# From block 3 on VectorE transposes q in 32x32 blocks, and x is made on 32x64 tiles of the TensorE array

## The chip, the core and the metric

One core of one Trainium2 chip. Its engines run on their own and meet through semaphores: TensorE (PE: matmuls; PEld: its weight loads), VectorE (DVE), ScalarE (ACT), GpSimd (POOL), and SyncE (SP), whose queue issues the transfers (DMA). The metric is device time in microseconds of one execution, as the median of several.

## What is computed

Attention of a linear kind, then a feed-forward layer:

```
q_s  = exp(q - max_d(q)) / sum_d                       # softmax over the 64 features
k_s  = exp(k - max_s(k)) / sum_s                       # softmax over the 576 positions
kv   = einsum('bhsd,bhse->bhde', k_s, v)               # 64x64 for each batch and head
x    = einsum('bhsd,bhde->bhse', q_s, kv)  -> (4608, 512)
out  = (h * sigmoid(1.702 h)) @ w_out,  h = x @ w_in   # 512 -> 2048 -> 512
```

There are 8 batches, 8 heads, 576 positions and 64 features. q, k and v are float32; the weights come as 64-bit floats and are split on the chip into two float32 parts.

## The kernel before

The 4608 tokens are cut into 12 blocks of 384 (TB), so that three blocks make two batches. A partition p of the 128 holds three tokens in a row (c = 0..2). Every other block of the later ones has tokens of two batches; `parts(t)` gives the one or two pieces.

For a block, **q** is loaded for one pair of heads at a time (`load_q`, from block 2 on into two buffers qt), made a softmax (`q_soft`: VectorE L532 maximum and L533 subtraction, ScalarE L536 exp, VectorE L539 to L542 sum, reciprocal and product), and turned so that features lie on partitions: `q_tr` has three TensorE transposes (L584) into a PSUM bank, and ScalarE copies them to qT (L591).

For a batch, **k** is made a softmax (`k_max`, `k_sub`), and `kv_pairs` multiplies it with v on TensorE (L494, 64 columns of the array for each head of a pair, 65 columns of data: the last is the sum). VectorE forms the reciprocals r (L499, L500), and ScalarE writes the scaled 64x64 blocks into kvn (L510), eight for a batch.

**x** is made by `x_pairs`. In blocks 0 to 2 it is one matmul of the full 128x128 array a head pair (L630), against kvn with zeros off the diagonal. From block 3 on all four head pairs go together on the four 64x64 tiles of the array (L635): four 64x64 products of two pairs fill the four tiles. For that, every second pair has its two heads exchanged (`turned`), which costs `load_q` two transfers in place of one. x is then split into a high and a low part, xh on ScalarE (L599) and xl on VectorE (L602).

**The feed-forward layer** is 16 steps a block: `g1` (L659: 12 matmuls of 384 columns, from xh, xl and two parts of w_in), gelu and a cast on ScalarE (L665, L668), the low part gl on VectorE (L671), and `g2` (L691: nine matmuls of 512 columns into three PSUM banks). g2 follows its g1 by two steps. The three results of a block are copied to tmp (L704) and stored (L707).

**The order** of every engine's list is fixed beforehand by a planner (`Plan`): each piece of work has a cost, the buffers that it reads and writes, and a rank; at each engine the ready piece of lowest rank goes next. The kernel then emits the pieces in that order, and each engine runs its list strictly in it. For blocks 2 and on, the ranks of loads, softmax, transposes and x are set by `n0(i)`, the sixteenths of the block ahead of it.

The weights' split (`conv_w`, L276 to L295) fills the first 150 us on VectorE and ScalarE. Early inputs of batches 0 and 1 lie in places where weights come later.

Of the kernel before, what the change touches and what calls it, by code (L numbers as in the profile page):

```python
# [131 lines left out]
def efficient_attention_then_gelu_ffn(  # L132
# [13 lines left out]
    nc = tc.nc  # L146
# [16 lines left out]
    QACT = set()  # L163
# [11 lines left out]
    kvn = [sb(f"kvn{i}", [P, NP, P]) for i in range(2)]  # L175
    xs = [[sb(f"x{s}{i}", [P, NP, TB], F32R) for s in "hl"] for i in range(2)]
    g = [sb(f"g{i}", [P, TB]) for i in range(3)]
# [5 lines left out]
    qt_ = [sb(f"qt{i}", [P, C, 2, D]) for i in range(2)]  # L183
    mx_ = [sb(f"mx{i}", [P, 2, D]) for i in range(2)]
# [4 lines left out]
    first = sb("first", [P, D])  # L189
    nc.vector.memset(first, 0.0)  # L190
    nc.gpsimd.partition_all_reduce(first, first, P, bass_isa.ReduceOp.max)
    for t in kvn:
        nc.vector.memset(t, 0.0)
# [3 lines left out]
    def zero_tail(kl, vl):  # L197
        nc.vector.memset(kl[ST:P], 0.0)
        nc.vector.memset(vl[ST:P], 0.0)
        nc.vector.memset(vl[:, :, D:W], 1.0)  # L200

    zero_tail(*tail[0])
    one = sb("one", [P, 1])
    nc.vector.memset(one, 1.0)
# [9 lines left out]
    for gr in range(2):  # L214
# [11 lines left out]
    et, _ = early("wi10", "et", [P, H * (D + W)], 0)  # L226
    etail[0] = (
        et[:, : H * D].rearrange("p (h d) -> p h d", h=H),
        et[:, H * D : H * (D + W)].rearrange("p (h d) -> p h d", h=H),
# [154 lines left out]
    def turned(b, hp):  # L384


        return b > 1 and hp % 2 == 1

    def load_q(t, i, rank):
        n = group(t)  # L390
        qt, key = eq[t, i] if t < 2 else (qt_[i % 2], ("qt", i % 2))
        qbuf[t, i] = qt, key
        runs = [(0, 1, 1), (1, 0, 1)] if turned(parts(t)[0][0], i) else [(0, 0, n)]

        def run():
            for b, s0, p0, p1 in parts(t):
                for o, h, m in runs:
                    src = q[b, n * i + h : n * i + h + m, s0 : s0 + (p1 - p0) * C, :]
                    if t < 2:
                        nc.sync.dma_start(  # L400
                            out=qt[p0:p1].rearrange("p h c d -> p h (c d)"),
                            in_=src.rearrange("h (p c) d -> p h (c d)", c=C),
                        )
                    else:
                        nc.sync.dma_start(
                            out=qt[p0:p1, :, o : o + m], in_=src.rearrange("h (p c) d -> p c h d", c=C)
                        )

        plan.add("SP", plan.ISSUE * len(parts(t)) * len(runs), behind(t > 1), (key,), rank, run, size=n * TB * D * 4)
# [4 lines left out]
    def k_max(b, i, rank):  # L414
# [4 lines left out]
        s = nm[0] % 2  # L419
# [48 lines left out]
    def kv_pairs(b, hps, t, rank):  # L468
# [12 lines left out]
        def run():  # L481
            for m, hp in enumerate(hps):
                i, o = divmod(2 * hp, n)
                kt, vt = kbuf[b, i][0], vbuf[b, i][0]

                for cols in (slice(0, D), slice(D, W)) if b < 2 else (slice(0, W),):
                    for c in range(CM + 1):
                        for a in range(2):
                            lhs = kt[:, o + a, c, :] if c < CM else kl[:, 2 * hp + a, :]
                            rhs = vt[:, o + a, c, :] if c < CM else vl[:, 2 * hp + a, cols]  # L490
                            if cols.start == D:
                                rhs = vl[:, 2 * hp + a, cols] if c == CM else one
                            r0 = (a ^ turned(b, hp)) * D
                            nc.tensor.matmul(  # L494
                                pk[r0 : r0 + D, m, cols], lhs, rhs, start=c == 0, stop=c == CM, tile_position=(0, r0)
                            )
# [7 lines left out]
        plan.add("DVE", 0.35, (PB,), (R,), rank, run_r)  # L504
        for m, hp in enumerate(hps):

            def run_n(m=m, hp=hp):
                for a in range(2):
                    rows, cols = (slice(x * D, (x + 1) * D) for x in (a ^ turned(b, hp), a))
                    nc.scalar.mul(kvn[b % 2][rows, hp, cols], pk[rows, m, 0:D], r[rows, m : m + 1])  # L510

            plan.add("ACT", 0.65, (PB, R), (("kvn", b % 2, hp),), rank, run_n)
# [3 lines left out]
    sums = [sb(f"qs{i}", [P, 4 * C]) for i in range(2)]  # L516
    qm = [sb(f"qm{i}", [P, 4 * C]) for i in range(2)]

    def q_soft(t, i, ranks):
# [25 lines left out]
        if (t, i) in QACT:  # L545

            flat = qt.rearrange("p h c d -> p (h c d)")
            mf, sf = qm[i % 2], sums[i % 2]

            def run_n():  # L550
                nc.vector.tensor_reduce(out=m, in_=qt, axis=AX.X, op=ALU.max, negate=True)

            def run_a():
                for x in range(n * C):
                    w = flat[:, x * D : (x + 1) * D]
                    nc.scalar.activation(w, w, AF.Exp, bias=mf[:, x : x + 1], accum_out=sf[:, x : x + 1])

            def run_z():
                nc.vector.tensor_scalar_add(sf, sf, 1e-9)
                nc.vector.reciprocal(sf, sf)  # L560
                nc.vector.tensor_tensor(
                    out=dst, in0=qt, in1=bc(sf.rearrange("p (h c) -> p h c", h=n), D), op=ALU.mult
                )

            Q = ("qs", i % 2)
            plan.add("DVE", dve(e), (key,), (M,), ranks[0], run_n)
            plan.add("ACT", 0.30 * n * C, (key, M), (key, Q), ranks[1], run_a, table="exp")
            plan.add("DVE", dve(e) + 0.4, (key, Q), (nkey, Q), ranks[2], run_z)
            return
# [5 lines left out]
    def q_tr(t, hp, rank):  # L575
        n = group(t)
        i, o = divmod(2 * hp, n)
        qt, key = qbuf[t, i]
        bk = next_bank(t)
# [8 lines left out]
        qT, Q = qTs[hp], ("qT", hp)  # L588

# [5 lines left out]
    def x_out(t, hp, px, PB, rank):  # L595
        xh, xl = (x[:, hp, :] for x in xs[t % 2])

        def run_h():
            nc.scalar.copy(xh, px[:, :TB])  # L599

        def run_l():
            nc.vector.tensor_tensor(out=xl, in0=px[:, :TB], in1=xh.bitcast(F32), op=ALU.subtract)  # L602

        X = ("x", t % 2)
        plan.add("ACT", act(TB), (PB,), ((*X, "h", hp),), rank, run_h)
        plan.add("DVE", dve(TB), (PB, (*X, "h", hp)), ((*X, "l", hp),), rank, run_l)

    def x_pairs(t, hps, rank):


        bks = [next_bank(t) for _ in hps[-3:]]
        if len(hps) > 3:

            bks.insert(0, 6 + (ng[0] + 1) % 2)
        reads = []
        for hp in hps:
            reads.append(("qT", hp))
            reads += [("kvn", b % 2, hp) for b, *_ in parts(t)]

        def run():  # L620
            for b, s0, p0, p1 in parts(t):
                todo = []
                for hp, bk in zip(hps, bks):
                    qx, po = (
                        y[:, :TB].rearrange("a (c p) -> a c p", c=C)[:, :, p0:p1] for y in (qTs[hp], bank[bk])
                    )
                    todo.append((po, kvn[b % 2][:, hp, :], qx, hp % 2))
                if len(hps) == 1:
                    (po, kx, qx, _), = todo
                    nc.tensor.matmul(po, kx, qx, start=True, stop=True)  # L630
                    continue
                for pair, a in ((y, a) for y in range(0, len(todo), 2) for a in range(2)):
                    for po, kx, qx, odd in todo[pair : pair + 2]:
                        ri, ro = (slice(y * D, (y + 1) * D) for y in (a ^ odd, a))
                        nc.tensor.matmul(  # L635
                            po[ro], kx[ri, ro], qx[ri], start=True, stop=True, tile_position=((a ^ odd) * D, a * D)
                        )

        PBs = [("bank", bk) for bk in bks]
        plan.add("PE", 0.67 if len(hps) == 1 else 1.64, reads, PBs, rank, run)  # L640
        for hp, bk, PB in zip(hps, bks, PBs):
            x_out(t, hp, bank[bk], PB, rank)
# [4 lines left out]
    def g1(t, j, rank):  # L647
# [5 lines left out]
        gt, (gh, gl) = g[n % 3], gs[n % 3]  # L653
# [20 lines left out]
        PB, G = ("bank", bk), ("g", n % 3)  # L674
        plan.add("PE", 2.1, (*X, (f"wi{j}", 0), (f"wi{j}", 1)), (PB,), rank, run)
        plan.add("ACT", act(TB), (PB,), (G,), rank, run_g, table="gelu")
        plan.add("ACT", act(TB), (G,), ((*G, "h"),), rank, run_h)
        plan.add("DVE", dve(TB), (G, (*G, "h")), ((*G, "l"),), rank, run_l)
# [73 lines left out]
    def attend(t, b, r, step):  # L752
        for i in range(2):
# [3 lines left out]
            for hp in (2 * i, 2 * i + 1):  # L757
                at(r + 3 * step, lambda rank, hp=hp: kv_pairs(b, (hp,), t, rank))
                at(r + 3 * step, q_tr, t, hp)
                at(r + 3.5 * step, x_pairs, t, (hp,))  # L760
# [11 lines left out]
    for t in range(2, NB):  # L772
# [34 lines left out]
    for rank, _, f, a in sorted(tasks, key=lambda s: s[:2]):  # L807
        if f in (load_k, load_v, load_q, k_max, k_sub, q_tr, x_pairs, g1, g2, load_w, conv_w, load_tail):
# [38 lines left out]
```

## Time and profile before

| | us |
|---|---|
| median of 3 runs | 904.86 (904.68 to 905.02) |
| profiled execution | 903.99, span 902.2 |
| TensorE busy | 878.6 (97% of the span) |
| ScalarE / VectorE busy | 501.3 / 387.5 |
| TensorE, the feed-forward matmuls alone (L659 and L691) | 88% of the chain that ended last |

A row of a timeline gives the start, the duration, engine and line, what is written and read, shapes and a count. Matmuls are pipelined: the next starts before the one before has ended, so the distance of starts tells what a matmul costs TensorE. A matmul of float32 data leaves two records, a transposition one. "PEld" rows are the weight loads. In a table of stretches come the length, then busy time and count for TensorE, its loads, VectorE, ScalarE and GpSimd, then the granted TensorE clock as a share of full speed, and what the transfers moved. A row for one line alone gives the shortest, median and longest duration in ns.

### The profile page before, as it was taken

The page shows a single profiled execution, that of the slowest core. Times are in us where ns is not written, and L with a number is a line of the kernel's source. Part 1 is how long each engine was busy: PE and PEld are TensorE (multiplying, and loading weights), DVE is VectorE, ACT ScalarE, POOL GpSimd, SP SyncE. Part 2 cuts the span into 40 slices and gives each one's busy share as a digit, 9 for nine tenths or more (in the row PEclk, how much of TensorE's full clock was granted, in tenths as well). Part 3 has the DMA queues.
Part 4 walks back from the last instruction along what each step waited for, and adds up shares of the span by engine and source line. Part 5 has one row for each costly group of instructions (what it writes and reads, how often), then busy time and mean ns, then how long its engine had stood idle before and what let it go on. Part 6 is the DMA issues. An engine that isn't in the chain of part 4 may idle for free.

```text
span 902.2 us, 13027 instructions
## 1 busy us (share of the span) xinstructions
PE 878.6 (97%) x5200; PEld 782.8 (87%) x5200; DVE 387.5 (43%) x826; ACT 501.3 (56%) x850; POOL 24.6 (3%) x35
## 2 busy tenths in 40 slices
PE   3899999999999999999999999999999999999998
PEld 3689999889899988989889889989988898988997
DVE  8999986344432631341641452332354133131111
ACT  3776668646843972652882693553495365253222
POOL 1100001000100100000100000000010000000000
PEclk9899999999999999999999999999999999999999
DMA  9995000113100410000500500000230000000000
GB/s 272 361 378 138 1 1 1 53 53 93 49 36 21 112 44 9 17 13 35 122 18 36 123 19 36 18 19 36 55 86 36 16 12 26 29 10 1 36 1 36
DMA packets 94620, 55.37 MB, mean 61 GB/s; under 512 B 67424, under 2 KB 87904, under 8 KB 94560
## 3 DMA queue, kind: packets, MB, share of 16 engines
q1 hardware_dynamic: 94560, 54.54, 20.9%
q8 instruction: 41, 0.67, 0.3%
q14 instruction: 19, 0.16, 0.1%
HBM read 45.09 MB, written 9.44 MB: 60 GB/s over the span
## 4 chain that ended last, share of the span: by engine, by line
PE 94%; DVE 4%; ACT 1%; DMA 0%; issue 0%; POOL 0%; ACTq 0%; DVEq 0%
PE bank L691 44%; PE bank L659 44%; PE bank L494 2%; PE bank L584 2%; PE bank L635 1%; PE bank L630 1%; DVE ek L447 1%; DMA ek<-in_k 0%; DVE en L542 0%; DVE eq L533 0%; DVE tmp L284 0%; DVE tmp L285 0%; DVE qm L539 0%; DVE qm L532 0%; ACT ek L453 0%; DVE em L426 0%
## 5 line engine op out<-in xcount | busy, mean ns | idle before, releaser
L659 PE MATMUL bank<-xh,w 128*128 128x384 f32 x1536 | 426.6, 340 | 0.0
L691 PE MATMUL bank<-w,gh 128*128 128x512 f32 x1152 | 364.0, 397 | 0.0
L659 PEld LDWEIGHTS bank<-xh,w 128*128 128x128 f32 x1536 | 281.8, 189 | 7.8 <-ACT g L665 0.3
L671 DVE TENSOR_TENSOR gl<-g,gh 128x384 fp32r<-128x384 f32 x192 | 106.6, 556 | 400.5 <-ACT gh L668 400.5
L659 PE MATMUL bank<-xl,w 128*128 128x384 f32 x768 | 259.4, 338 | 2.4 <-DVE xl L602 2.4
L665 ACT ACTIVATE g<-bank 128x384 f32<-128x384 f32 x192 | 94.4, 492 | 290.3 <-PE bank L659 289.0
L691 PEld LDWEIGHTS bank<-w,gh 128*128 128x128 f32 x1152 | 213.2, 188 | 40.2 <-issue 4.4
L691 PE MATMUL bank<-w,gl 128*128 128x512 f32 x576 | 227.9, 396 | 0.0
L659 PEld LDWEIGHTS bank<-xl,w 128*128 128x128 f32 x768 | 145.2, 189 | 10.1 <-DVE xl L602 2.7
L691 PEld LDWEIGHTS bank<-w,gl 128*128 128x128 f32 x576 | 108.3, 188 | 24.9
L668 ACT CAST gh<-g 128x384 fp32r<-128x384 f32 x192 | 98.4, 513 | 6.5 <-PE bank L691 0.7
L665 ACT ACT_TABLE_LOAD x59 | 75.7, 1283 | 1.1
L536 ACT ACT_TABLE_LOAD x39 | 50.0, 1283 | 0.7
L591 ACT COPY qT<-bank 128x384 f32<-128x384 f32 x48 | 22.6, 478 | 34.1 <-PE bank L584 34.0
L539 DVE TENSOR_REDUCE qm<-qt 128x6 f32<-128x384 f32 x40 | 22.0, 550 | 36.1 <-ACT qt L536 36.1
L532 DVE TENSOR_REDUCE qm<-qt 128x6 f32<-128x384 f32 x40 | 21.9, 549 | 31.3 <-DMA qt<-in_q 31.3
L432 POOL PARTITION_ALL_REDUCE mx<-mx x24 | 18.6, 776 | 603.8 <-DVE mx L428 603.8
L453 ACT ACT_TABLE_LOAD x20 | 25.7, 1283 | 5.6 <-DMA ek<-in_k 5.3
L289 ACT CAST w<-tmp 128x512 fp32r<-128x512 f32 x32 | 19.5, 618 | 14.2 <-DVE tmp L285 11.0
L276 ACT ACTIVATE tmp<-raw 128x512 f32<-128x512 f32 x32 | 21.2, 676 | 7.2 <-DVE w L295 4.5
L602 DVE TENSOR_TENSOR xl<-bank,xh 128x384 fp32r<-128x384 f32 x48 | 24.1, 550 | 2.4 <-ACT xh L599 2.3
L510 ACT ACTIVATE kvn<-bank,r 64x64 f32<-64x64 f32 x64 | 17.8, 305 | 12.7 <-DVE r L500 11.6
(71 smaller groups left out, 481.9 us busy)
## 6 DMA issues: line engine op xcount, KB each, us to landing
out<-tmp SPq DMA_DIRECT2D x36, 256.0 KB, 2.1
raw<-in_moe_w_in SPq DMA_DIRECT2D x16, 512.0 KB, 10.4
raw<-in_moe_w_out SPq DMA_DIRECT2D x16, 512.0 KB, 9.4
kt<-in_k SPq DMA_DIRECT2D x24, 256.0 KB, 4.1
vt<-in_v SPq DMA_DIRECT2D x48, 128.0 KB, 4.0
qt<-in_q SPq DMA_DIRECT2D x36, 96.0 KB, 2.7
qt<-in_q SPq DMA_DIRECT2D x16, 192.0 KB, 2.9
ek<-in_k SPq DMA_DIRECT2D x4, 512.0 KB, 6.9
```

The source lines that it names most:

```text
L276: nc.scalar.activation(ff, words()[:, :, 1].bitcast(F32), AF.Copy, scale=2.0**-112)
L453: nc.scalar.activation(t, t, AF.Exp)
L532: nc.vector.tensor_reduce(out=m, in_=qt, axis=AX.X, op=ALU.max)
L536: nc.scalar.activation(qt, qt, AF.Exp)
L539: nc.vector.tensor_reduce(out=m, in_=qt, axis=AX.X, op=ALU.add)
L591: nc.scalar.copy(qT, pq[:, :TB])
L602: nc.vector.tensor_tensor(out=xl, in0=px[:, :TB], in1=xh.bitcast(F32), op=ALU.subtract)
L659: nc.tensor.matmul(ph, wi[w][j][:, c, :], x[:, c, :], start=c == 0 and i == 0, stop=c == KC - 1 and i == 2,)
L665: nc.scalar.activation(gt, ph, AF.Gelu_apprx_sigmoid)
L668: nc.scalar.copy(gh, gt)
L671: nc.vector.tensor_tensor(out=gl, in0=gt, in1=gh.bitcast(F32), op=ALU.subtract)
L691: nc.tensor.matmul(po[c], x[:, cs], wo[w][j], start=j == 0 and i == 0, stop=j == NJ - 1 and i == 2)
```

## The change

Blocks 0 to 2 keep their way of making x (now `x_pair`). From block 3 on:

- `q_tr` is one VectorE instruction, a transposition in 32x32 blocks of the whole 128x384 tile, straight into qT. Within each quarter of 32 partitions (32 times three tokens), qT then holds features on partitions, in pieces of 32.
- `x_all` multiplies each quarter with its own copy of kv: for each head pair, each half e of the features, each quarter y of the partitions and each head a of the pair, one matmul on the 32x64 tile at row 32y and column 64a, 96 columns of data; the two halves e add up in PSUM. 64 matmuls in place of 8 (or 16). Each quarter has its bank.
- `kv_pairs` for batches 2 to 7 writes the scaled result once with VectorE (into m1) and sends it to kvq, four copies, in 16 transfers on SP; ScalarE's eight scalings go.
- no pair is `turned`, so `load_q` is one transfer for each piece of a block.
- buffers: one qt and one mx in place of two, two g in place of three (with their own key in the planner), kvn shares space with the kvq of even batches, `first` and `one` become parts of other tiles.
- the ranks of q's loads, softmax and transposes move: head pair hp is loaded at `n0(3 hp)`, made a softmax at `n0(3 hp + 1)` and turned at `n0(3 hp + 2)`, in block 2 as well.

```diff
-    g = [sb(f"g{i}", [P, TB]) for i in range(3)]
+    g = [sb(f"g{i}", [P, TB]) for i in range(2)]
...
-    qt_ = [sb(f"qt{i}", [P, C, 2, D]) for i in range(2)]
-    mx_ = [sb(f"mx{i}", [P, 2, D]) for i in range(2)]
+    qt_ = [sb("qt", [P, C, 2, D])]
+    mx_ = [sb("mx", [P, 2, D])]
...
+        if b > 1:
+            st = m1_.rearrange("p (m d) -> p m d", d=D)
+            def run_st():
+                nc.vector.tensor_tensor(out=st, in0=pk[:, :, 0:D], in1=bc(r, D), op=ALU.mult)
+            def run_q():
+                kvq[b] = sb(f"kvq{b}", [P, NP, 2, 2, D], tag=f"kvq{b % 2}" if b % 2 else "kvn")
+                for y in range(4):
+                    for a in range(2):
+                        for e in range(2):
+                            nc.sync.dma_start(
+                                out=kvq[b][y * Q4 : (y + 1) * Q4, :, a, e, :],
+                                in_=st[a * D + e * Q4 : a * D + (e + 1) * Q4],
+                            )
...
+            plan.add("DVE", dve(NP * D), (PB, R), (("m1", True),), rank, run_st)
+            plan.add("SP", 16 * 0.6, (("m1", True),), (("kvq", b % 2), *old), rank, run_q, size=4 * P * NP * D * 4)
+            return
...
+        if t > 2:
+            def run_t():
+                nc.vector.transpose(out=qT, in_=qt.rearrange("p c h d -> p (c h d)"))
+            plan.add("DVE", dve(TB), (key,), (Q,), rank, run_t)
+            return
...
+    def x_all(t, rank):
+        bks = [6 + (ng[0] + 1) % 2] + [3 * (t % 2) + y for y in range(3)]
+        reads = [("qT", hp) for hp in range(NP)] + [("kvq", b % 2) for b, *_ in parts(t)]
+        def run():
+            for hp in range(NP):
+                qv = qTs[hp].rearrange("p (c a e t) -> p c a e t", c=C, a=2, e=2)
+                for e in range(2):
+                    for y in range(4):
+                        rows = slice(y * Q4, (y + 1) * Q4)
+                        b = next(b for b, _, p0, p1 in parts(t) if p0 <= y * Q4 < p1)
+                        for a in range(2):
+                            po = bank[bks[y]][a * D : (a + 1) * D, hp * C * Q4 : (hp + 1) * C * Q4]
+                            nc.tensor.matmul(
+                                po.rearrange("p (c t) -> p c t", c=C), kvq[b][rows, hp, a, e, :], qv[rows, :, a, e, :],
+                                start=e == 0, stop=e == 1, tile_position=(y * Q4, a * D),
+                            )
+        PBs = [("bank", bk) for bk in bks]
+        plan.add("PE", 1.64, reads, PBs, rank, run)
...
-                ld = n0(5 + d) + 0.1 if gq else n0(0) - (7 if t == 2 else 3) + d
+                ld = n0(0) - (7 if t == 2 else 3)
...
-                at(ld + 0.2, load_q, t, hp)
-                at(n0(i0 + 1 + d), lambda rank, t=t, hp=hp: q_soft(t, hp, (rank, rank, rank)))
-                at(n0(i0 + 5 + d), q_tr, t, hp)
+                at(n0(3 * hp) if hp else ld + 0.2, load_q, t, hp)
+                at(n0(3 * hp + 1), lambda rank, t=t, hp=hp: q_soft(t, hp, (rank, rank, rank)))
+                at(n0(3 * hp + 2), q_tr, t, hp)
                 if t == 2:
-                    at(n0(i0 + 6 + d), x_pairs, t, (hp,))
+                    at(n0(i0 + 6 + d), x_pair, t, hp)
                 elif hp == NP - 1:
-                    at(n0(i0 + 6 + d), x_pairs, t, range(NP))
+                    at(n0(i0 + 6 + d), x_all, t)
```

The lists of two engines show where block 2's q stands. On TensorE, before the change, from the third transposition of block 2 (L584, `q_tr`; L630 is its x, L691 is g2):

```order
L584 MATMUL bank_62<-ident,qt_100 128x128 x3
L691 MATMUL bank_66<-w,gh_79 128x512 x2
L691 MATMUL bank_66<-w,gl_80 128x512
L691 MATMUL bank_64<-w,gh_81 128x512 x2
L691 MATMUL bank_64<-w,gl_82 128x512
L630 MATMUL bank_63<-qT_98,kvn_71 128x384
L584 MATMUL bank_61<-ident,qt_101 128x128 x3
L691 MATMUL bank_65<-w,gh_81 128x512 x2
L691 MATMUL bank_65<-w,gl_82 128x512
L691 MATMUL bank_66<-w,gh_81 128x512 x2
L691 MATMUL bank_66<-w,gl_82 128x512
L630 MATMUL bank_62<-qT_99,kvn_71 128x384
```

And after the change, from the same transposition (now L582; L612 is x, L489 is `kv_pairs` of batch 2):

```order
L582 MATMUL bank_62<-ident,qt 128x128 x3
L489 MATMUL bank_64<-vt_90,kt_86 64x65 x8
L489 MATMUL bank_64<-vl_102,kl_101 64x65 x2
L489 MATMUL bank_64<-vt_91,kt_87 64x65 x8
L489 MATMUL bank_64<-vl_102,kl_101 64x65 x2
L489 MATMUL bank_64<-vt_92,kt_88 64x65 x8
L489 MATMUL bank_64<-vl_102,kl_101 64x65 x2
L489 MATMUL bank_64<-vt_93,kt_89 64x65 x8
L489 MATMUL bank_64<-vl_102,kl_101 64x65 x2
L612 MATMUL bank_61<-qT_96,kvn 128x384
L582 MATMUL bank_63<-ident,qt 128x128 x3
L612 MATMUL bank_62<-qT_97,kvn 128x384
```

Before, the two transpositions read two buffers (qt_100, qt_101); now both read qt, the work between them is kv_pairs of batch 2, and the last x follows its transposition directly.

On SP before the change, around the stores of block 0 (L707), and behind them the loads of q (L405): the last two head pairs of block 2, then the first of block 3:

```order
L707 DMA out<-tmp_85 128x512
L707 DMA out<-tmp_86 128x512
L707 DMA out<-tmp_87 128x512
L405 DMA qt_100<-in_q 128x6x64
L405 DMA qt_101<-in_q 128x6x64
L405 DMA qt_100<-in_q 128x6x64
```

And after (L401 are loads of q, the last three head pairs of block 2; L713 are stores, the first of block 0, the others of block 1):

```order
L401 DMA qt<-in_q 128x6x64
L713 DMA out<-tmp_85 128x512
L401 DMA qt<-in_q 128x6x64
L713 DMA out<-tmp_83 128x512
L713 DMA out<-tmp_84 128x512
L401 DMA qt<-in_q 128x6x64
L713 DMA out<-tmp_85 128x512
```

The last load of block 2's q now stands behind two stores of block 1, and each load waits until the one buffer has been turned.

The x matmuls of block 3, after the change, are 64 of this kind on TensorE; the row of two is one quarter's pair of heads, and the four rows are the four quarters (before: eight of 64x384):

```order
L697 MATMUL bank_63<-w,gl_82 128x512
L634 MATMUL bank_68<-qT_94,kvq_1702 64x96 x2
L634 MATMUL bank_64<-qT_94,kvq_1702 64x96 x2
L634 MATMUL bank_65<-qT_94,kvq_1702 64x96 x2
L634 MATMUL bank_66<-qT_94,kvq_1702 64x96 x2
```

These four rows repeat for the second half of the features, and then for each further head pair.

More of the change, by code (lines that the diff above doesn't have):

```diff
@@ L174, in efficient_attention_then_gelu_ffn @@
     ident = sb("ident", [P, P])
-    kvn = [sb(f"kvn{i}", [P, NP, P]) for i in range(2)]
+    kvn_ = sb("kvn", [P, 2, NP, P])
+    kvn = [kvn_[:, i] for i in range(2)]
+    kvq = {}
+    Q4 = P // 4
     xs = [[sb(f"x{s}{i}", [P, NP, TB], F32R) for s in "hl"] for i in range(2)]
-    g = [sb(f"g{i}", [P, TB]) for i in range(3)]
+    g = [sb(f"g{i}", [P, TB]) for i in range(2)]
     gs = [[sb(f"g{s}{i}", [P, TB], F32R) for s in "hl"] for i in range(LAG + 1)]
@@ L544, in q_soft @@
         e = n * C * D
[L545 to L569, printed above, removed]
         plan.add("DVE", 2 * dve(e), (key,), (key, M), ranks[0], run_m)
@@ L604, in x_out @@
         X = ("x", t % 2)
[L605 to L618, printed above, removed]
+        plan.add("ACT", act(TB), (PB,), ((*X, "h", n),), rank, run_h)
@@ L620, in run, with x_pair @@
+        plan.add("DVE", dve(TB), (PB, (*X, "h", n)), ((*X, "l", n),), rank, run_l)
+    def x_pair(t, hp, rank):
+        bk = next_bank(t)
+        px = bank[bk][:, :TB]
+        reads = [("qT", hp)] + [("kvn", b % 2, hp) for b, *_ in parts(t)]
         def run():
+            qv, pv = (y.rearrange("a (c p) -> a c p", c=C) for y in (qTs[hp], px))
             for b, s0, p0, p1 in parts(t):
[L622 to L637, printed above, removed]
@@ L639, in x_pairs, with view @@
[L639 to L642 removed]
+                nc.tensor.matmul(pv[:, :, p0:p1], kvn[b % 2][:, hp, :], qv[:, :, p0:p1], start=True, stop=True)
+        PB = ("bank", bk)
+        plan.add("PE", 0.67, reads, (PB,), rank, run)
+        x_out(t, hp, px, lambda x: x[:, hp, :], PB, rank)
+    def x_all(t, rank):
[13 more added lines that the diff above has]
+                                start=e == 0, stop=e == 1, tile_position=(y * Q4, a * D),
+                            )
+        PBs = [("bank", bk) for bk in bks]
+        plan.add("PE", 1.64, reads, PBs, rank, run)
+        for y, bk in enumerate(bks):
+            src = bank[bk][:, :TB].rearrange("p (h c t) -> p h c t", h=NP, c=C)
+            def view(x, y=y):
+                x = x.rearrange("p h (c y t) -> p h c y t", c=C, y=4)
+                return x[:, :, :, y, :]
+            x_out(t, y, src, view, PBs[y], rank)
@@ L673, in g1 @@
         X = [("x", t % 2, s, hp) for s in "hl" for hp in range(NP)]
-        PB, G = ("bank", bk), ("g", n % 3)
+        PB, F, G = ("bank", bk), ("gf", n % 2), ("g", n % 3)
         plan.add("PE", 2.1, (*X, (f"wi{j}", 0), (f"wi{j}", 1)), (PB,), rank, run)
-        plan.add("ACT", act(TB), (PB,), (G,), rank, run_g, table="gelu")
-        plan.add("ACT", act(TB), (G,), ((*G, "h"),), rank, run_h)
-        plan.add("DVE", dve(TB), (G, (*G, "h")), ((*G, "l"),), rank, run_l)
+        plan.add("ACT", act(TB), (PB,), (F,), rank, run_g, table="gelu")
+        plan.add("ACT", act(TB), (F,), ((*G, "h"),), rank, run_h)
+        plan.add("DVE", dve(TB), (F, (*G, "h")), ((*G, "l"),), rank, run_l)
     def g2(t, j, rank):
@@ L759, in attend @@
                 at(r + 3 * step, q_tr, t, hp)
[L760 removed]
+                at(r + 3.5 * step, x_pair, t, hp)
             r += 2 * step
```

70 lines of the change are left out of this document (31 added, 39 removed).

## The prediction

> **What bounds the kernel now.** I read the shares of the page first, then its chain of work that ended last.
>
> ```profile
> PE 878.6 (97%) x5200; PEld 782.8 (87%) x5200; DVE 387.5 (43%) x826; ACT 501.3 (56%) x850; POOL 24.6 (3%) x35
> ...
> PE 94%; DVE 4%; ACT 1%; DMA 0%; issue 0%; POOL 0%; ACTq 0%; DVEq 0%
> PE bank L691 44%; PE bank L659 44%; PE bank L494 2%; PE bank L584 2%; PE bank L635 1%; PE bank L630 1%; DVE ek L447 1%; DMA ek<-in_k 0%; DVE en L542 0%; DVE eq L533 0%; DVE tmp L284 0%; DVE tmp L285 0%; DVE qm L539 0%; DVE qm L532 0%; ACT ek L453 0%; DVE em L426 0%
> ```
>
> TensorE is the chain: 94% of it. From about 60 us on its list runs without a hole, so a microsecond taken off that list there is a microsecond of the end, and work moved to VectorE or to a queue costs only if TensorE comes to wait for it. The stretch table says how much room the others have in a later block:
>
> ```profile
> 345.00:415.00 70.00, 70.00 (x367) 62.22 (x366) 21.39 (x45) 32.83 (x54) 0.00 (x0) 1.00 0.08 23
> ```
>
> TensorE is busy for 70.00 of 70 us, VectorE (third pair) for 21.39, ScalarE for 32.83.
>
> **What the change takes away: the transposes on TensorE.** First a plain place in the timeline of TensorE, then one with a transposition (start, duration):
>
> ```profile
> 231.08 0.39 PE L691 MATMUL bank<-w,gl 128*128 128x512 f32 x1
> 231.31 0.34 PE L659 MATMUL bank<-xh,w 128*128 128x384 f32 x1
> 231.48 0.34 PE L659 MATMUL bank<-xl,w 128*128 128x384 f32 x1
> ...
> 235.26 0.40 PE L691 MATMUL bank<-w,gl 128*128 128x512 f32 x1
> 235.50 0.49 PE L584 MATMUL bank<-ident,qt 128*128 128x128 f32 x3
> 235.75 0.43 PE L659 MATMUL bank<-xh,w 128*128 128x384 f32 x1
> 236.01 0.34 PE L659 MATMUL bank<-xl,w 128*128 128x384 f32 x1
> ```
>
> Matmuls overlap, so starts count, not durations. The three transposes take 235.75 - 235.50 = 0.25 us, and the matmul after them holds the next one back for 0.26 instead of 0.17: 0.335 us per head pair. They go in blocks 3 to 11, four a block: 36 x 0.335 = **-12.1 us**. The 36 copies into qT (L591) leave ScalarE too, worth nothing there. VectorE gets 36 transposes; nearest are its passes over the same 128x384 (0.55 us, L532 below), so 2.2 us a block in an engine idle for 48 of 70 us. Even four times that hides.
>
> **x on 32x64 tiles.** The present form, and its weight loads:
>
> ```profile
> 245.25 0.63 PE L691 MATMUL bank<-w,gh 128*128 128x512 f32 x2
> 245.71 0.39 PE L691 MATMUL bank<-w,gl 128*128 128x512 f32 x1
> 246.03 1.52 PE L635 MATMUL bank<-qT,kvn 64*64 64x384 f32 x16
> 247.48 0.73 PE L691 MATMUL bank<-w,gh 128*128 128x512 f32 x2
> 248.05 0.39 PE L691 MATMUL bank<-w,gl 128*128 128x512 f32 x1
> ...
> 319.26 1.53 PE L635 MATMUL bank<-qT,kvn 64*64 64x192 f32 x32
> ```
> ```profile
> 246.03 0.21 PEld L635 LDWEIGHTS bank<-qT,kvn 64*64 64x64 f32 x8 [0.36 <-issue]
> 246.41 0.15 PEld L635 LDWEIGHTS bank<-qT,kvn 64*64 64x64 f32 x4 [0.17 <-issue]
> 246.73 0.15 PEld L635 LDWEIGHTS bank<-qT,kvn 64*64 64x64 f32 x4 [0.17 <-issue]
> ```
>
> Eight matmuls leave 16 records, two each. They go in rounds of four, one per tile, 0.32 us apart (246.41, 246.73): 1.28 us. It starts 0.09 us late (245.71 to 246.03 where 0.23 is usual), takes 1.45 to the next start and delays the one after by 0.10 (0.57 for 0.46): 1.64 us in all, 0.36 of it entry and exit. The new form has 64 matmuls of 96 columns, so 128 records on eight tiles: 16 rounds of 0.32 x 96/384 = 0.08 us, again 1.28. The row of 32 records with half the columns costs 0.01 us more than that of 16; I take twice that and a little, 0.03 us more a block, 9 x 0.03 = **+0.3 us**. That needs eight tiles at work at once, which no row here shows. Bound from above: the smallest matmuls in the trace, with one column,
>
> ```profile
> 57.38 0.58 PE L494 MATMUL bank<-one,ek 128*64 128x1 f32 x16
> 57.82 0.26 PE L494 MATMUL bank<-vl,kl 128*64 128x1 f32 x4
> ```
>
> come every 0.44/16 = 0.0275 us on two tiles. 128 at that pace are 3.5 us, 2.2 more a block, +20 us. Below there is little: 1.28 is what the columns need, so at best -0.3 us in sum. I take the low end, since the pace of rounds follows the columns in both L635 rows.
>
> **A new wait in block 2.** Block 2 keeps its TensorE transposes, but q now has one buffer. A load waits for the transposes of the head pair before; on TensorE's list the last two transposes have only kv_pairs and one x between them. The chain behind a load, as it ran with two buffers:
>
> ```profile
> 170.26 13.21 SPq L405 DMA_DIRECT2D qt<-in_q  x5
> ...
> 173.31 0.55 DVE L532 TENSOR_REDUCE qm<-qt 128x6 f32<-128x384 f32 x1 [3.84 <-DMA qt<-in_q]
> ...
> 173.97 0.56 DVE L533 TENSOR_TENSOR qt<-qt,qm 128x384 f32<-128x384 f32 x1
> ...
> 175.79 0.53 ACT L536 ACTIVATE qt<-qt 128x384 f32<-128x384 f32 x1
> ...
> 176.90 0.54 DVE L539 TENSOR_REDUCE qm<-qt 128x6 f32<-128x384 f32 x1
> ...
> 177.90 0.56 DVE L542 TENSOR_TENSOR qt<-qt,qm 128x384 f32<-128x384 f32 x1
> ```
>
> Load to first reduction 3.05 us; reduction and subtraction 1.22 (173.31 to 174.53); exp 0.53; sum to product 176.90 to 178.46 = 1.56; three hand-overs of some 0.07: 6.6 us. The load also stands behind a store on SP whose copy ends just before (about 0.6 us, one issue): 7.1 us from the end of the transposes. Meanwhile TensorE has
>
> ```profile
> 214.16 2.48 PE bank L494 x80
> ```
> ```profile
> 181.09 0.81 PE L630 MATMUL bank<-qT,kvn 128*128 128x384 f32 x2
> 181.74 0.49 PE L584 MATMUL bank<-ident,qt 128*128 128x128 f32 x3
> 181.98 0.71 PE L691 MATMUL bank<-w,gh 128*128 128x512 f32 x2
> ...
> 182.31 0.49 ACT L591 COPY qT<-bank 128x384 f32<-128x384 f32 x1
> ```
>
> kv_pairs 2.48 and one x 0.65: 3.1 us. It idles 7.1 - 3.1 = 4.0 us. Then x of the last pair waits for its copy: transposes 181.74, copy done 182.80, TensorE free from 181.98; about 0.7 us now that nothing stands between. **+4.7 us**, between 4.0 (no store in the way) and 6.5 (a table load of 1.28 in the chain and VectorE busy). Queued behind the waiting transposes is all of TensorE's list. The first feed-forward matmuls of block 2 then use the three older pairs' x, so the last pair's eviction hides. The earlier pairs have 9 us of matmuls between their transposes.
>
> **The clock after that wait.** The longest hole on TensorE once x of block 0 is made, and the granted clock around it:
>
> ```profile
> 34.55 0.44 PE L659 MATMUL bank<-xl,w 128*128 128x384 f32 x1 [2.45 <-DVE xl L602]
> ```
> ```profile
> 32.00:35.00 3.00, 0.55 (x3) 0.45 (x3) 2.86 (x6) 1.50 (x3) 0.00 (x0) 1.00 1.09 377
> 35.00:38.00 3.00, 2.40 (x28) 1.90 (x27) 3.00 (x6) 2.32 (x3) 0.00 (x0) 0.50 1.05 372
> 38.00:41.00 3.00, 3.00 (x28) 2.99 (x27) 2.56 (x8) 2.73 (x7) 0.00 (x0) 0.50 1.10 349
> 41.00:42.00 1.00, 1.00 (x5) 1.00 (x5) 1.00 (x2) 0.98 (x2) 0.94 (x1) 0.60 1.10 349
> ```
>
> After 2.45 us of idling the granted clock (the 0.50 behind the busy times) halved from about 35.0 to 41.8, 6.8 us. A wait of 4.0 us is longer, so I count one such dip: half of 6.8 us is lost, **+3.4 us**. [...]
>
> **Costed at nothing.** The state for blocks 3 on: one VectorE product and 16 SP copies replace eight ScalarE scalings.
>
> ```profile
> L405 SPq DMA_DIRECT2D qt<-in_q x76: 540/606/3009, 60.8 to 791.9; - x76
> ```
>
> 16 issues of 0.61 are 9.7 us, plus 1 us on VectorE and some 3 us to land: 14 us, while 13 half steps of 2.1 us (27 us) stand between kv_pairs and x on TensorE's list. Without that cover the difference would be a hole in each of six batches. SP's later loads move back by 10 us in blocks of 70. One q buffer in later blocks: a round of 7 to 8 us four times a block of 70. Two g instead of three: gelu now waits for the gl two steps back, which the matmuls two steps on need anyhow. One mx and the shared m1 put VectorE's next k maximum behind the 16 copies; queued behind it are gl passes, for which TensorE's second matmuls wait two steps (8 us) later, and by then the 14 us have passed.
>
> **Sum.** -12.1 + 0.3 + 4.7 + 3.4 = -3.7 us. The profiled execution took 903.99 us (span 902.2 and 1.8 around it), 0.87 below the median of 904.86: 900.3 there, **901.2 us** as a median.
>
> **Rivals.**
> 1. The array doesn't run eight tiles at once. For it: no row shows more than four. Against: both L635 rows follow their columns. With four at once 16 rounds become 32, 1.28 us more a block: 901.2 + 9 x 1.25 = 912.4; at the pace of the one-column rows 921. From 0.4 us a block on the gain is gone. Chance 0.20, three quarters of it slower. [...]
> 2. No dip of the clock: 897.8. [...] 0.14.
> 3. No wait in block 2 because the load comes sooner: 904.86 - 12.1 + 0.3 = 893.1. Against: the issue-to-reduction time of 3.05 alone fills TensorE's cover of 3.1. 0.06.
> 4. A second wait, of one half step (2.1 us) or two, from the shared buffers (early stage, where VectorE is busiest, or SP's longer list): 903 to 905. 0.12.
>
> The forecast keeps 0.48, with its own range 899 to 903. A measurement tells 0.2% (1.8 us) from no change. Faster: 0.48 + 0.14 + 0.06, less the forecast's upper edge: 0.67. Same, between 903.1 and 906.7: case 4, that edge, and a mild case 1: 0.17. Slower: the rest of case 1 and a hard case 4: 0.16. The range 896.5 to 909 leaves out case 3 and the heavy part of case 1.
>
> **What the new profile would show.** No transposes on TensorE after some 195 us, and 36 transposes of about 0.55 us on VectorE. The x row at about 1.55 us for 128 records; 2 us or more is rival 1. A hole of about 4 us before the last transposes, near 188 us, released by VectorE, then 0.50 in the clock for 6 to 7 us. Elsewhere no TensorE wait over 0.5 us; waits on kvq copies, or on gl in the stage from 60 to 100 us, would make me wrong.

## The result, and the profile after

| | before | after |
|---|---|---|
| median, us | 904.90 (904.68 to 905.02, 4 runs) | 910.35 (908.87 to 910.80, 4 runs) |
| profiled execution: time, span | 903.99, 902.2 | 910.55, 908.8 |
| TensorE busy | 878.6 | 877.9 |
| VectorE / ScalarE busy | 387.5 / 501.3 | 412.4 / 486.9 |

The ratio is 1.0054, with a 95% interval of 1.0042 to 1.0066: slower, by 5.45 us. I had forecast 901.2, in a range from 896.5 to 909.0.

The first part of the page after, and its chain of work that ended last (L665 and L697 are the feed-forward matmuls g1 and g2, L634 the new x, L612 the old x of blocks 0 to 2, L489 `kv_pairs`):

```profile
PE 877.9 (97%) x6052; PEld 785.2 (86%) x6052; DVE 412.4 (45%) x865; ACT 486.9 (54%) x776; POOL 24.0 (3%) x35
...
PE 93%; DVE 3%; SPq 1%; DMA 1%; ACT 1%; issue 0%; DVEq 0%; ACTq 0%
PE bank L697 44%; PE bank L665 44%; PE bank L489 2%; PE bank L634 2%; DMA raw<-in_moe_w_out 1%; PE bank L612 1%; PE bank L582 1%; SPq L362 0%; DVE tmp L288 0%; DVE tmp L287 0%; DVE w L298 0%; DVE qm L554 0%; DVE qm L547 0%; DVE ek L441 0%; DVE en L557 0%
```

TensorE is still the chain, and it is busy for as long as before, though 108 transposition matmuls have gone. So something on its own list takes longer. In the view of waits, TensorE waits for nothing after 205 us.

Most of what I expected is there. The groups of VectorE by form (instructions, busy us and mean ns, idle time before) show the 36 transpositions at 0.58 us, near the 0.55 that I took:

```profile
L573 DVE STREAM_TRANSPOSE qT<-qt 128x384 f32<-128x384 f32 x36 | 20.8, 578 | 7.8 <-PE bank L634 6.8
```

The timeline of TensorE in block 2 shows the new wait where I had put it, and the table of stretches behind it the half clock (the number behind the busy times):

```profile
190.00 0.91 PE L612 MATMUL bank<-qT,kvn 128*128 128x384 f32 x2
194.31 0.90 PE L582 MATMUL bank<-ident,qt 128*128 128x128 f32 x3 [3.40 <-DVE qt L557]
195.78 1.65 PE L612 MATMUL bank<-qT,kvn 128*128 128x384 f32 x2 [0.57 <-ACT qT L587]
```
```profile
193.00:200.00 7.00, 5.12 (x14) 4.12 (x15) 1.71 (x5) 2.24 (x3) 0.00 (x0) 0.55 0.92 238
200.00:201.00 1.00, 1.00 (x5) 1.00 (x5) 0.27 (x1) 0.00 (x0) 0.00 (x0) 0.71 0.98 220
```

Two waits of 3.40 and 0.57 us make 4.0 us. A mean clock of 0.55 over 7 us and of 0.71 over 1 us is some 6.9 us at half; 1.1 us of it TensorE idled anyway, so it lost about 2.9.

Two things are not as I expected. The first is x. Its rows in the timeline (start, duration), in a block whose quarters belong to two batches, and in one whose quarters all read a fresh kvq (blocks with two batches are every third one, here 4, 7 and 10, not every other as I wrote above):

```profile
327.98 1.88 PE L634 MATMUL bank<-qT,kvq 32*64 32x96 f32 x128
329.78 0.73 PE L697 MATMUL bank<-w,gh 128*128 128x512 f32 x2
...
469.32 2.13 PE L634 MATMUL bank<-qT,kvq 32*64 32x96 f32 x128
471.38 0.74 PE L697 MATMUL bank<-w,gh 128*128 128x512 f32 x2
```

From start to the next matmul's start it takes 1.80 and 2.06 us; the old form took 1.45. Over nine blocks, from the last matmul ahead of x to the third behind it, the starts add up to 20.70 us before and 24.46 after: +3.8 us.

The second is the pace of everything else. The chain of waits over a stretch of the last block, where neither kernel has any other work on TensorE, merges each g1 (12 matmuls) and each g2 (nine) into a piece (start, length). Before, and after:

```profile
847.96 2.08 PE bank L659 x12
850.04 2.10 PE bank L691 x9
852.14 2.08 PE bank L659 x12
854.22 2.10 PE bank L691 x9
856.32 2.08 PE bank L659 x12
```
```profile
858.15 2.12 PE bank L665 x12
860.27 2.11 PE bank L697 x9
862.38 2.12 PE bank L665 x12
864.49 2.11 PE bank L697 x9
866.60 2.12 PE bank L665 x12
```

One step (g1 and g2) took 4.18 us before and takes 4.23 here, with the clock at 1.00 in both. The change touches neither g1's nor g2's matmuls. From the first matmul of the second step of the last block to that of the fourteenth, twelve steps, it is 50.18 us before and 50.50 after.

The n-th matmul of g1 is the same work in both traces, so their starts can be subtracted. After minus before: +1.8 us at the 25th matmul (52 us), +2.8 at the 361st (170 us), +9.3 at the 529th (block 2 is past), +6.25 at the 2257th (877 us). The wait and the dip stand in block 2, as forecast; but the nine blocks behind it give back only 3 us, where I had expected 11.8.

### The profile page after: what moved, and what is told of

Its sections match the earlier page's. It is cut to its first block, busy times and chain, and to the rows that moved or that the text cites. A ratio compares the mean times of both kernels' runs of the same rounds, so it can differ in the third digit from the quotient of the medians.

```text
span 908.8 us, 14732 instructions
## 1 busy us (share of the span) xinstructions
PE 877.9 (97%) x6052; PEld 785.2 (86%) x6052; DVE 412.4 (45%) x865; ACT 486.9 (54%) x776; POOL 24.0 (3%) x35
## 4 chain that ended last, share of the span: by engine, by line
PE 93%; DVE 3%; SPq 1%; DMA 1%; ACT 1%; issue 0%; DVEq 0%; ACTq 0%
PE bank L697 44%; PE bank L665 44%; PE bank L489 2%; PE bank L634 2%; DMA raw<-in_moe_w_out 1%; PE bank L612 1%; PE bank L582 1%; SPq L362 0%; DVE tmp L288 0%; DVE tmp L287 0%; DVE w L298 0%; DVE qm L554 0%; DVE qm L547 0%; DVE ek L441 0%; DVE en L557 0%
## 5 line engine op out<-in xcount | busy, mean ns | idle before, releaser
L665 PE MATMUL bank<-xh,w 128*128 128x384 f32 x1536 | 427.8, 340 | 0.0
L697 PE MATMUL bank<-w,gh 128*128 128x512 f32 x1152 | 365.2, 398 | 0.6 <-DVE w L298 0.6
L665 PEld LDWEIGHTS bank<-xh,w 128*128 128x128 f32 x1536 | 282.7, 189 | 9.6 <-ACT g L671 0.6
L665 PE MATMUL bank<-xl,w 128*128 128x384 f32 x768 | 260.5, 339 | 2.5 <-DVE xl L598 2.5
L697 PEld LDWEIGHTS bank<-w,gh 128*128 128x128 f32 x1152 | 213.8, 188 | 38.8 <-DVE w L298 1.4
L697 PE MATMUL bank<-w,gl 128*128 128x512 f32 x576 | 227.6, 395 | 0.0
L665 PEld LDWEIGHTS bank<-xl,w 128*128 128x128 f32 x768 | 145.0, 189 | 10.5 <-DVE xl L598 2.7
L697 PEld LDWEIGHTS bank<-w,gl 128*128 128x128 f32 x576 | 108.3, 188 | 26.4 <-DVE gl L677 0.3
L595 ACT CAST xh<-bank 128x384 fp32r<-128x384 f32 x48 | 20.2, 489 | 12.5 <-PE bank L612 6.9
L489 PE MATMUL bank<-ev,ek 128*64 128x64 f32 x128 | 7.7, 285 | 18.2 <-DMA raw<-in_moe_w_in 14.5
```

The lines of the kernel that those rows point to most:

```text
L489: nc.tensor.matmul(pk[r0 : r0 + D, m, cols], lhs, rhs, start=c == 0, stop=c == CM, tile_position=(0, r0))
L665: nc.tensor.matmul(ph, wi[w][j][:, c, :], x[:, c, :], start=c == 0 and i == 0, stop=c == KC - 1 and i == 2,)
L697: nc.tensor.matmul(po[c], x[:, cs], wo[w][j], start=j == 0 and i == 0, stop=j == NJ - 1 and i == 2)
```

## The experiments

Each ratio is to executions of the kernel before that were taken alongside; their medians were 904.78 to 905.19 us.

### Block 2

The changed kernel, with a second q buffer for block 2 alone, in space that is free then, and the old ranks there:

```
+    qt2 = sb("qt2", [P, C, 2, D], tag="kvq1")
...
+        if t == 2 and i % 2:
+            qt, key = qt2, ("kvq", 1)
...
+                if t == 2:
+                    at((n0(5 + d) + 0.1 if gq else ld + d) + 0.2, load_q, t, hp)
+                    at(n0(i0 + 1 + d), lambda rank, t=t, hp=hp: q_soft(t, hp, (rank, rank, rank)))
+                    at(n0(i0 + 5 + d), q_tr, t, hp)
```

> The changed kernel with block 2 as it was: two buffers for q (the second shares the space of the odd kvq, which is free until batch 3) and the old ranks for loads, softmax and transposes of block 2; the rest is as changed. Theory: the wait of 3.4 + 0.6 us before the last transposes of block 2 and the half clock behind it go, 6.5 us: 904, with no stretch at half clock after 50 us. Rival: the wait moves to another place (the clock falls there too), and less than 2 us are gained: 908.5 or more.

Measured: 903.22 us, ratio to before 0.9978 (0.9967 to 0.9988). The stretch in which the changed kernel waited, in the table of stretches of this one:

```profile
190.00:200.00 10.00, 10.00 (x55) 9.32 (x54) 5.83 (x14) 8.10 (x12) 0.00 (x0) 1.00 0.30 96
```

TensorE is busy throughout and the clock stays at 1.00. By the starts of the same matmuls of g1, 0.3 us have been gained at the 361st and 7.3 at the 481st, and behind it no more than 0.2 changes. So the wait and its dip cost 7.0 us, and the theory holds.

### What sets the time of x

Three runs change only the 64 matmuls of x. First, half of the columns:

```
-    po.rearrange("p (c t) -> p c t", c=C), kvq[b][rows, hp, a, e, :], qv[rows, :, a, e, :],
+    po.rearrange("p (c t) -> p c t", c=C)[:, :, : Q4 // 2],
+    kvq[b][rows, hp, a, e, :], qv[rows, :, a, e, : Q4 // 2],
```

> The changed kernel in which each matmul of the new x has 48 columns of data in place of 96 (half of the tokens are left out); the number of matmuls and weight loads is the same. Theory (the columns set the pace of x, as I predicted): from the first to the last start x falls from 1.6 to 1.9 us to about 0.8, 9 blocks by 0.9 are 8 us: 902. Rival (issue or weight loads set it): x stays at 1.5 to 1.9 us, and the time within 1.5 us of 910.4.

Then another order of the matmuls, in the kernel with two buffers in block 2:

```
-                    for y in range(4):
-                        for a in range(2):
+                    for a in range(2):
+                        for y in range(4):
```

> The changed kernel with two buffers in block 2 (903.2 us), and the 64 matmuls of the new x in another order: the four quarters run innermost, then the two heads, so neighbours go to different rows of the array and the same columns. If the array's tiles work independently and the rate of issue or of weight loads sets the pace, x stays at 1.6 to 1.9 us from first to last start and the time within 1 us of 903.2. If neighbours that share rows get in each other's way now, x falls towards 1.3 us: 3 to 4 us less, 899.5.

And half of the weights, in the kernel of the section below whose weights all stand 288 bytes above x:

```
-    po = bank[bks[y]][a * D : (a + 1) * D, hp * C * Q4 : (hp + 1) * C * Q4]
+    po = bank[bks[y]][a * D : a * D + Q4, hp * C * Q4 : (hp + 1) * C * Q4]
...
-    kvq[b][rows, hp, a, e, :], qv[rows, :, a, e, :],
+    kvq[b][rows, hp, a, e, :Q4], qv[rows, :, a, e, :],
```

> The run with all weights 288 bytes above x and gh (895.3 us; x 1.59 to 1.89 us from first to last start), with one change: each matmul of the new x has 32 columns of weights in place of 64 (half of the features of x are left out); 64 matmuls, 96 columns of data and 128 records stay. If the length of a weight load sets the pace of x, it falls by a fifth or more, to 1.0 to 1.3 us: 892 or less. If the number of instructions sets it, x stays at 1.55 to 1.9 us and the time within 1 us of 895.3.

Rows of TensorE's timeline for x in block 5, with half of the columns, and with half of the weights (in the changed kernel the same x starts at 397.32, and the next matmul at 399.08):

```profile
396.16 1.54 PE L634 MATMUL bank<-qT,kvq 32*64 32x48 f32 x128
397.63 0.73 PE L698 MATMUL bank<-w,gh 128*128 128x512 f32 x2
```
```profile
386.78 1.72 PE L639 MATMUL bank<-qT,kvq 32*32 32x96 f32 x128
388.43 0.72 PE L702 MATMUL bank<-w,gh 128*128 128x512 f32 x2
```

| x of one block, first to last start, us | blocks 3, 6, 9 | 4, 7, 10 | 5, 8, 11 |
|---|---|---|---|
| as changed | 1.89 | 1.64 | 1.59 |
| half of the columns | 1.68 | 1.39 | 1.32 |
| half of the weights | 1.79 | 1.54 | 1.48 |
| quarters innermost | 1.89 | 1.59 | 1.59 |

Half of the columns takes off 0.21 to 0.27 us where "columns set the pace" wanted 0.8; half of the weights takes off 0.10; the order changes only blocks 4, 7 and 10, by 0.05. The times, one execution each, were 907.47 (1.45 us ahead by its first g1 already; neither side of its expectation), 902.65 and 895.27 us. What is left when either is halved are 128 weight loads and 128 matmuls, 256 instructions in 1.3 to 1.9 us, or 5 to 7 ns each. So the number of instructions is what fits; no run halved it, so this is argued and not shown.

It is not that eight tiles can't work at once. The table of stretches for L634 alone, the first 0.1 us of x in block 5 (length, busy time and count of TensorE and of its loads, clock):

```profile
397.30:397.40 0.10, 0.08 (x8) 0.08 (x12) 1.00 0.00 0
```

Eight matmuls start within the first 0.08 us, and by the records each of them lasts 0.29 us, so all eight are under way together. The second round of eight comes 0.13 us later, the third and the fourth 83 ns each, as I had worked out. From the fifth round on the starts thin out to 12 ns a matmul and more.

### Where the tiles lie

A step of g1 and g2 reads the weights and the tiles x or gh. In every kernel here x and gh have one remainder to 512 bytes in a partition (it differs from kernel to kernel), and all offsets within these tiles are multiples of 512 bytes. So I counted how far the weights stand above x and gh, to 512 bytes. The built programs say: 18 of the 32 weight tiles (those that early inputs share) 448 and the other 14 at 288 before the change; 160 and 352 after. The change did this in passing: `first` (256 bytes) and `one` (a slot of 32) no longer stand ahead of the weights, and behind the 18 some small tiles are gone or shorter.

First the kernel before with those two edits alone:

```
-    first = sb("first", [P, D])
+    first = m1_[:, 0:D]
...
-    one = sb("one", [P, 1])
-    nc.vector.memset(one, 1.0)
+    one = tail[0][1][:, 0, D:W]
```

> The kernel before, with only two of the change's edits: the tile first is a part of m1, the tile one a part of vl. 288 bytes go ahead of the weights, so the 18 weight tiles get the remainder to 512 bytes that they have in the changed kernel; nothing else of the work changes but one memset. Theory A (pace by place): steps rise from 4.18 to 4.20 to 4.23, 12 blocks of 16 steps, 3 to 6 us: 908 to 911. Theory B (pace by program or chip): 904.9, within 0.5. If the start of the changed kernel (the first matmul 2.2 us later) comes from the folded tiles, the first matmul of the feed-forward layer starts at 32.5 instead of 30.4; if it is chance or another edit, at 30.4.

Measured: 908.87 us, ratio 1.0040 (1.0028 to 1.0053), in size three quarters of the change's net loss. The chain of waits in the last block of this kernel, whose work is that of before:

```profile
860.42 2.12 PE bank L658 x12
862.53 2.07 PE bank L690 x9
864.61 2.12 PE bank L658 x12
866.73 2.08 PE bank L690 x9
868.81 2.11 PE bank L658 x12
```

g1 has gone from 2.08 to 2.12, though every matmul and its order are as they were. From the 25th to the 2257th matmul of g1 it takes 828.25 us, and 824.72 before: +3.5 us from place alone.

Then the changed kernel with four small tiles moved ahead of the weights (all 32 then stand 352 above):

```
+    rs = [sb(f"r{i}", [P, NP]) for i in range(2)]
+    qm = [sb(f"qm{i}", [P, 4 * C]) for i in range(2)]
     held = {}
     def early(tag, name, shape, batch):
...
-    rs = [sb(f"r{i}", [P, NP]) for i in range(2)]
-    qm = [sb(f"qm{i}", [P, 4 * C]) for i in range(2)]
```

> The changed kernel with the four small tiles of the softmax sums (192 bytes for each partition) laid out ahead of the 18 weight tiles that early inputs share, instead of behind them; the program is the same, only addresses move. Theory A (the pace of the ordinary matmuls follows where the tiles lie): those 18 tiles now have the same remainder to 512 bytes as the other 14, whose steps of g1 and g2 took 4.19 us; ten of sixteen steps a block fall from 4.22 to 4.19, some 4 us in all: 906. Theory B (the slower pace comes from the program or from the chip, not from addresses): steps stay at 4.22 and the time at 910.4, within 0.5.

Measured: 908.14 us, 1.0032 (1.0019 to 1.0044). Between the same matmuls it is 1.7 us faster, so places matter here too, but I had the sizes wrong: with all weights at one distance the steps alternate, 4.185 and 4.215, each second one slow.

The next four go by the distance. The first two have two buffers in block 2; the edit of the second is shown, the others move the same small tiles and the 18 early ones to other places:

```
+    rs = [sb(f"r{i}", [P, NP]) for i in range(2)]
     xs = [[sb(f"x{s}{i}", [P, NP, TB], F32R) for s in "hl"] for i in range(2)]
...
+    qm = [sb(f"qm{i}", [P, 4 * C]) for i in range(2)]
     held = {}
```

> The changed kernel with block 2 as in the run before (two buffers there, 903.2 us), and with the tiles laid out so that the weights stand to x and to gh as in the kernel before: 18 weight tiles 64 bytes below them to 512, 14 tiles 288 bytes above. The program is the same, addresses alone differ. Theory A (the distance of the weights from the moving tiles, to 512 bytes, sets the pace): every step is back at 4.18 us, 5 us in all: 898. Theory A' (the remainder of the weights' own address decides, here 128 and 480): steps of 4.19 and 4.21, as those remainders had elsewhere: 902 or more. Theory B (not addresses): 903.2.

> As the run with the layout of before, but all 32 weight tiles 288 bytes above x and gh to 512 (remainder 480). Theory A (distance): the steps are those that the kernel before has with its 14 tiles, 4.17 to 4.19: 898 to 899. Theory A' (own remainder): steps alternate between 4.185 and 4.215 as with all tiles at 480: 901.5. Theory B: 903.2.

Measured: 897.27 us, 0.9915 (0.9902 to 0.9929), and 895.28, 0.9895 (0.9881 to 0.9908), against 903.22 for the same program in the old places. Among these kernels the distance decides, not the weights' own remainder: at a remainder of 480 all weights go by 4.173 here, and by 4.185 and 4.215 with the small tiles first. The chain of waits in the last block with all at 288:

```profile
838.66 2.09 PE bank L670 x12
840.75 2.08 PE bank L702 x9
842.83 2.09 PE bank L670 x12
844.92 2.08 PE bank L702 x9
847.01 2.09 PE bank L670 x12
```

Steps of 4.17 us: in the blocks from 3 on, all that hold no other work lie between 4.168 and 4.174. Both kernels were faster than I had said, by 1 and 3 us. Part of that is the pace, which I had counted at 5 us: from the 25th to the 2257th matmul of g1 it is 822.29 us in the old places, 816.84 in those of before (5.5 less), and 815.70 with all at 288 (6.6 less).

Then the kernel before with its weights at 288, and the change as it was made, with its one buffer, in the places of before:

> The kernel before with small tiles moved in the layout (first and one folded, the wi10 tile 32 bytes shorter, as in the change) so that all 32 weight tiles stand 288 bytes above x and gh to 512; its work stays as it was. If the distance sets the pace whatever the program, steps go from 4.181 to 4.173 us, 190 steps by 8 ns = 1.5 us: 903.4 against 904.9. Then the change's own part, at one placement and without its wait in block 2, is 895.3 - 903.4 = -8.1 (36 transposes -11.8, x +3.7). Rival: 288 is good for the changed program alone, and this one stays at 904.9 or goes above.

> The changed kernel with its one q buffer and its wait in block 2, and the tiles laid out so that weights stand to x and gh as in the kernel before (64 bytes below for 18, 288 above for 14, to 512). If wait and pace add up: 910.35 - 5.9 = 904.4, no change against the kernel before within 0.2%; steps of 4.173 to 4.194 us, the half clock behind the wait of block 2 stays. Rival: the two share time (a slower pace hid a part of the wait), and it is over 905.5 or under 903.

Measured: 904.34, ratio 0.9995 (0.9986 to 1.0004), and 903.74, ratio 0.9991 (0.9982 to 1.0000). The first gains 0.9 us between the same matmuls, which the times don't tell from nothing. The second is the change without its accident: its wait and the half clock are there, in its timeline and its stretches,

```profile
191.63 0.60 PE L583 MATMUL bank<-ident,qt 128*128 128x128 f32 x3 [3.38 <-DVE qt L558]
```
```profile
192.00:199.00 7.00, 6.43 (x20) 5.59 (x19) 1.29 (x3) 2.88 (x5) 0.00 (x0) 0.51 0.92 226
```

and yet it comes out no slower than before. Wait and pace add up to within 0.5 us: from the 25th to the 2257th matmul of g1, wait and dip cost 824.23 - 816.84 = 7.4 us in these places and 829.20 - 822.29 = 6.9 in the change's own. At one distance (288) and without the wait, the change is worth 895.28 - 904.34 = -9.1 us by the medians, and 815.70 - 823.82 = -8.1 between the same matmuls.

Two neighbouring distances, one execution each:

> As the run with all weights 288 bytes above x and gh (895.3 us, steps of 4.173), but 256 above. If the pace changes with every 32 bytes, steps are elsewhere, up to 4.23: 895 to 905. If the remainder to 64 alone counts (0 in place of 32), as at distance 0: steps of about 4.19, 898.5.

> As the run with all weights 288 bytes above x and gh (895.3 us, steps of 4.173), but 320 above. If the pace changes with every 32 bytes: between that and the alternating 4.185 and 4.215 at 352, 896 to 901. If the remainder to 64 alone counts, the same as at 256.

Measured: 898.26 and 894.69 us. At 256 the steps are 4.186 throughout. At 320 there are three paces in one layout, 4.147, 4.167 and 4.187; each holds until other work passes, and then it can change. The chain of waits in block 6 at 320, around `kv_pairs` (L497):

```profile
493.10 2.07 PE bank L703 x9
495.17 2.12 PE bank L671 x12
497.28 2.07 PE bank L703 x9
499.35 2.49 PE bank L497 x80
501.84 2.29 PE bank L671 x12
504.12 2.06 PE bank L703 x9
506.19 2.08 PE bank L671 x12
```

Ahead of it g1 takes 2.12, behind it 2.08. So the distance alone doesn't fix the pace at 320. The last block, in the table, is one of the slow stretches there; between the 25th and the 2257th matmul of g1 this trace takes 814.22 us, the least of all.

| distance of the weights (18, 14 tiles) | kernels | twelve steps of the last block, us |
|---|---|---|
| 448, 288 | before; the change in these places; the same with two buffers | 50.18, 50.18, 50.18 |
| 160, 352 | the change; with two buffers; half columns; other order of x | 50.50, 50.50, 50.50, 50.50 |
| 288 | changed with two buffers; the same, half weights; before | 50.08, 50.08, 50.08 |
| 160, 0 | before with two tiles folded | 50.39 |
| 352 | the change, small tiles first | 50.40 |
| 256; 320 | changed with two buffers | 50.24; 50.24 |

Kernels with different programs and one layout agree to 0.01 us; one program in different layouts differs by 0.4 us in 50. That the distance counts to 512 bytes is enough to order these kernels; whether a shorter period would do was not tested.

## Why the prediction was wrong, point by point

**The transpositions** (-12.1 us) were right. In the kernel before at distance 288, where a plain step is 4.173 us, the six steps of block 7 that hold a transposition or stand next to one take 1.355 us more, 0.339 us for each of four.

**x on 32x64 tiles** was mis-sized: +0.3 us predicted, +3.8 measured, 0.30 to 0.34 us in six blocks and 0.60 in three. I took "the low end, since the pace of rounds follows the columns in both L635 rows". Those rows had 16 or 32 records in four tiles; at 128 records in eight the columns alone no longer set the pace (half of them took off 0.21 to 0.27 us a block, not 0.8). The upper bound from the one-column rows (2.2 us a block) was an honest bound; I went to its far end on the strength of two rows that had no small matmul in them. Rival 1 gave a wrong reason (eight tiles do run at once) and the right direction: its threshold was 0.4 us a block, and the mean is 0.42.

Eight tiles at once stand in the trace: the first records of eight tiles (0.29 us long, the second ones 0.24) start within 0.08 us, and the last record of x starts 1.59 to 1.89 us after the first.

**The wait in block 2** (+4.7) was 4.0, and **the clock behind it** (+3.4) was 2.9, since 1.1 of the 6.9 us at half clock were idle. Both were at their place, with the releasers that I had named, and undoing block 2 gave back 7.0 of the 8.1. Rivals 2 and 3 (no dip, no wait) fall. For the dip I had gone by the row of this kernel, where 2.45 us of idling halved the clock. The four traces with a wait of 3.4 us (the change, small tiles first, half of the columns, the places of before) all show it: a mean clock of 0.50 to 0.55 over the 4 to 7 us from about its end on.

**Costed at nothing**: this held. After 205 us TensorE waits for no kvq copy, no gl, no q buffer. Rival 4 (a second wait) falls.

**The step that was not there.** I wrote of the small edits of the layout (`first`, `one`, the shared buffers) only as edits, and compared matmuls by the rows of before, as if 0.17 and 0.23 us belonged to the instruction. So the sum put the pace of the feed-forward matmuls at no change, without a reason. It belongs to the instruction and its place. Between the same two matmuls of g1, the change's program in its own places takes longer than in those of before: 5.0 us as it was made (829.20 - 824.23), 5.5 with two buffers in block 2. By the medians, that turned a difference of -1.0 us (903.74 against 904.78) into +5.45.

**The sum** over the trace, from the 25th to the 2257th matmul of g1: -12.2 (transpositions, 36 x 0.339) + 3.8 (x) + 7.0 (block 2) + 5.5 (pace) = +4.1; the two traces differ there by 829.20 - 824.72 = +4.5. The first three, which are the prediction's own terms, make -1.4, where I had -3.7: x is 3.5 worse and block 2 is 1.1 better than I said. So even with the old places the forecast of 901.2 would have been some 2 us low, for the sake of x; the rest of the miss is the pace.

**The start.** The profiled execution of the change stood 1.8 us behind before it had done anything new. The transfers of v in SP's timeline, before, after, and in the change at the places of before:

```profile
4.70 1.87 SPq L359 DMA_DIRECT2D ev<-in_v  x2
```
```profile
4.84 4.23 SPq L362 DMA_DIRECT2D ev<-in_v  x2
```
```profile
4.71 1.83 SPq L365 DMA_DIRECT2D ev<-in_v  x2
```

Two issues took 4.23 us in one execution, 1.83 in another with the same list of work. In the eleven profiled executions with this start the first matmul of g1 began between 30.31 and 32.57 us. The change with half of the columns of x has the same addresses and the same list up to there, and began at 31.12 where the change began at 32.57; the kernel before with the two folded tiles began at 31.05, neither of the two starts that I had set against each other. So the start varies from execution to execution without a change of place or work; how much of it is in the medians stays open.

## What to carry to other kernels

When a change adds, drops or resizes a tile, even a slot of 32 bytes, compare the addresses of the operands of the matmuls that fill the time, before costing anything else: here 32 bytes of distance, from 288 to 256, took a step from 4.173 to 4.186 us, 288 bytes cost the kernel before 0.4%, and moving a few small tiles gave the changed one 0.8% (from 0.9978 to 0.9895 of the time before). Compare a plain stretch that the change doesn't touch first; if its pace has moved, an experiment with the old layout is the one that tells the change's worth. And price many small matmuls by the nearest row with many small matmuls in it, not by a row whose few large ones happen to scale with their columns.

## What the runs showed of the hardware

- **The pace of full-size fp32r matmuls went with the distance, to 512 bytes, between their two operands** (the weights, which are stationary in g1 and moving in g2, and x or gh): 4.15 to 4.23 us for 21 matmuls at clock 1.00, and for twelve steps of the last block 50.08 us at 288, 50.18 at 448 and 288, 50.50 at 160 and 352. In most of the layouts one step that follows no other work is steady to 1 to 3 ns from block to block. At 352 one distance gives two paces by turns (4.185 and 4.215), at 320 three that change when other work passes (4.147, 4.167 and 4.187), so the distance is not all that counts. What in the chip does it was not found.
- **Eight tiles of 32x64 do run at once**, but not for long: the third and the fourth round of eight came 83 ns after the one before, the average over 128 matmuls was 12 to 15 ns each instead of 10.
- **x cost 0.3 us more where all its kvq was fresh** (blocks 3, 6 and 9, 1.89 us against 1.59): there 16 of its weight loads carry a wait and 20 matmuls a signal, against 9 and 9 in the next blocks and 1 and 5 (4 in the last) in those after. The copies had landed over 10 us before: the last of each 16 was issued by 209.3, 453.9 and 668.3 us and no copy took over 3.7 us to land, and x starts at 253.6, 469.3 and 682.9. With the quarters innermost the next blocks (4, 7 and 10) have 9 waits and 7 signals, and x takes 1.59 us, the same as behind one wait and five signals; so the waits cost nothing there that shows. What a signal costs was not measured, and no run took waits or signals away in blocks 3, 6 and 9, so the cause of their 0.3 us was not shown.
- **A wait of 3.4 us on TensorE halved its clock for 6.8 to 6.9 us**, in all four traces that have it; in the kernel before 2.45 us of idling did so for 6.8 us.
